# Expert 0's weights fetched in 16 half pieces through two buffers, and the operand copies of the attention stage issued later

## The chip, the cores and the metric

The kernel runs on one core of a Trainium2 chip, as one launch. The metric is the device time of one execution in microseconds (us). TensorE is called PE below, VectorE DVE, ScalarE ACT, GpSimd POOL and SyncE SP; SP's own queue issues nearly all transfers of the stage in question.

## The reference

Three layers follow one another. The first is causal attention of 4 batches with 8 heads, 576 positions and 64 features, whose scores get a bias made from a running sum of `max(s, 0)`:

```python
cum = np.cumsum(np.maximum(s, 0.0), axis=-1)
bias = -(cum[:, :, :, None] - cum[:, :, None, :])
scores = np.where(causal, -1000000000.0, scale * q @ k.T + np.minimum(bias, 0.0))
attn = np.exp(scores - scores.max(-1)); attn = attn / (attn.sum(-1) + 1e-09)
out = attn @ v
```

Its output, 2304 tokens of 512 features, goes through a mixture of 8 experts: each token takes the expert of its largest gate logit, computes `relu(x @ w1[e]) @ w2[e]` (512 to 1024 to 512) and is scaled by two gates. The last layer is `relu(x @ w_in)**2 @ w_out` (512 to 2048 to 512). All inputs are float32, and w_in and w_out arrive as 64-bit words that the kernel converts itself.

## The kernel before

**Attention.** The 32 heads are worked on two at a time, so there are 16 pairs, numbered 0 to 15 here. A pair has seven units (a block of 128 queries of one or both heads, or the last 64 queries of both, the tail unit). For each unit PE multiplies queries with keys (`emit_s`, line 472), DVE adds the mask and finds the maximum (`emit_m`), ACT takes the exponentials (`emit_e`), PE transposes them (`emit_t`), ACT or DVE copies them out of PSUM (`emit_v`), and PE multiplies with the values (`emit_pv`).

**Operand tiles.** Queries and keys are held as a rounded part and a remainder, each a float32r number. For pairs from 2 on, ACT and DVE write both parts of both heads into one tile `sta` (three buffers, used in turn). Three transfers then copy head 1's rows into a second tile `stb` (two buffers), `spread_b`; after them two transfers overwrite the copied rows of `sta` with head 0's rows, `spread_a`. Four small transfers (`load_aug`) bring the bias rows into both tiles. The first score product of a pair needs the end of all of these. Since `spread_a` writes rows that `spread_b` reads, it may be issued only when the moves of `spread_b` have landed.

**What sets the order.** Every step is put into a list with a due time in units, seven per pair, and the list is sorted by it (`at`, `emit_tasks`). The sorted order is the program's order on every engine and queue; a due time is not a time on the chip. The numbers in the table `K_` are these due times. Of them `dup` is the due time of `spread_b` and `dupa` that of `spread_a`, both counted from the start of the pair ahead (`t0`):

```python
tb = t0 + max(K_["dup"], K_["qk"][2] + K_["qkl"] - early(pp) + 0.4)
at(tb - 0.05, load_aug, pp, 1)
at(tb, spread_b, pp)
at(tb - K_["dup"] + K_["dupa"], spread_a, pp)
```

For each pair SP issues, beside these, three transfers of values (line 362 and 365), four of raw queries and keys two to three pairs ahead (335 and 338), and two that store the attention's output of an earlier pair (708 and 712). SP works in order: a transfer that waits holds up all behind it.

**Expert 0's weights.** During pairs 8 to 15 the kernel also prepares the weights of the first expert, 4 MB in 8 pieces of 512 KB. Each is fetched into the buffer `stg` (line 224, one buffer of 128x1024), rounded by ACT into the first half of the weight tile (233), and POOL subtracts this from the raw piece to get the remainder (237). A piece is due every 6.88 units, its transfer 3.5 units ahead of ACT's cast. ACT works in order too, so that a cast that waits for its piece holds up the exponentials behind it.

The experts and the last layer follow; there the weights of later experts are prepared with other buffers and by DVE. `w_lo` and `w_job` serve both stages.

Of the kernel before, what the change touches and what calls it, by code (L numbers as in the profile page):

```python
# [12 lines left out]
F32 = mybir.dt.float32  # L13
# [6 lines left out]
ALU = mybir.AluOpType  # L20
# [4 lines left out]
P = 128  # L25
# [4 lines left out]
K_ = dict(  # L30
    S=3,
    O=0,
    pbufs=4,
    NO=5,
    od=[-1.86, -0.33],
    lorder=[0, 2, 11, 10, 3, 1, 4],
    lvact=[[0], [1], [0], [1], [1], [0], [1, 0]],
    lpv=[[7.65, 7.66], [4.06, 5.56, 6.05, 6.9, 7.45]],
# [17 lines left out]
    qk=[-3.45, -2.16, -1.89],  # L56
    qkh=0.61,
    qkl=0.65,
    dup=-3.2,
    dupa=-0.7,  # L60
    pv=[[3.74, 3.87], [8.47, 8.49, 8.51, 8.53, 8.57]],
    ovact=[1, 1],
    gk=[4.59, 4.65, 5.02, 5.22, 5.65, 6.55, 7.35, 7.38, 7.54, 8.68, 9.78, 10.48, 10.95, 11.72, 12.72, 14.11, 14.46, 14.36, 14.48, 14.97, 15.87, 16.25, 17.18, 17.4, 19.12, 20.76],
# [5 lines left out]
    w0=6.88,  # L69
# [17 lines left out]
def attention_moe_ffn_kernel(  # L87
# [14 lines left out]
    nc = tc.nc  # L102
# [9 lines left out]
    NPAIR = B * HP  # L112
# [50 lines left out]
    halves = {}  # L163
# [18 lines left out]
    def raw_src(key, i):  # L182
        e, ab = key
        if ab == "a":
            if e == 0:
                return w1[e, i * P:(i + 1) * P, :]
            if e < E:
                return w1.rearrange("e k f -> (e k) f")[ds(reg_e[e] * DM + i * P, P), :]
            c = (e - E) * FE
            return w_in[i * P:(i + 1) * P, c:c + FE]  # L190
        r = 2 * i * P
        if e == 0:
            return w2[e, r:r + 2 * P, :].rearrange("(k p) d -> p k d", p=P)
        if e < E:
            return w2.rearrange("e f d -> (e f) d")[ds(reg_e[e] * FE + r, 2 * P), :].rearrange("(k p) d -> p k d", p=P)
        r += (e - E) * FE
        return w_out[r:r + 2 * P, :].rearrange("(k p) d -> p k d", p=P)
# [11 lines left out]
    def at(key, fn, *args):  # L209
        tasks.append((key, len(tasks), fn, args))  # L210

    def emit_tasks(before=None):
        tasks.sort(key=lambda t: (t[0], t[1]))
        while tasks and (before is None or tasks[0][0] < before):
            _, _, fn, args = tasks.pop(0)
            fn(*args)

    raw = {}
# [8 lines left out]
    def w_parts(job):  # L227
        key, i = job
        w = halves[key]
        return w[:, 0, i * 1024:(i + 1) * 1024], w[:, 1, i * 1024:(i + 1) * 1024]  # L230
# [3 lines left out]

    def w_lo(job):
        hi, lo = w_parts(job)
        (nc.gpsimd if job[0][0] == 0 else nc.vector).tensor_tensor(out=lo, in0=raw.pop(job), in1=hi.bitcast(F32), op=ALU.subtract)  # L237

    def w_job(job, t_load, t_hi, t_lo):
        if job not in raw:  # L240
            at(t_load, w_load, job)
        at(t_hi, w_hi, job)
        at(t_lo, w_lo, job)

    def half_jobs(e, ab):
        return [((e, ab), i) for i in range(4)]
# [31 lines left out]
    with tc.manual_schedule():  # L278
        with ExitStack() as actx:
# [1 line left out]
            cq_p = actx.enter_context(tc.tile_pool(name="cq", bufs=1))  # L281
            qk_p = actx.enter_context(tc.tile_pool(name="qk", bufs=2))
            qr_p = actx.enter_context(tc.tile_pool(name="qr", bufs=1))
            stg_p = actx.enter_context(tc.tile_pool(name="stg0", bufs=1))
            v_p = actx.enter_context(tc.tile_pool(name="v", bufs=3))
            p_p = actx.enter_context(tc.tile_pool(name="p", bufs=K_["pbufs"]))
            sm_p = actx.enter_context(tc.tile_pool(name="sm", bufs=6))
# [583 lines left out]
            with tc.tile_pool(name="prep", bufs=1) as prep:  # L871
# [19 lines left out]
                    out=mf, in_=zf[:, 0:P], pattern=[[-1, P]], compare_op=ALU.is_ge, fill=NEG, base=0,  # L891
                    channel_multiplier=1)
                nc.vector.tensor_copy(out=mask[:, 3 * P:4 * P], in_=mf)
                for hd in range(2):
# [4 lines left out]
                    out=mt, in_=of[:, 0:P], pattern=[[1, P]], compare_op=ALU.is_gt, fill=0.0, base=0,  # L899
# [5 lines left out]
                    out=sel.unsqueeze(2), in_=ident.rearrange("p (g r) -> p r g", r=NH)[:, 0:2 * ND], axis=AX.X, op=ALU.add)  # L905
                nc.vector.tensor_scalar(out=sq, in0=sq, scalar1=0.0, scalar2=None, op0=ALU.max)
                nc.vector.tensor_tensor_scan(
                    out=cum, data0=cum_r[0:NH].bitcast(F32), data1=sq, initial=0.0, op0=ALU.mult, op1=ALU.add)
# [5 lines left out]
                    out=cum_k[NH:2 * NH], in0=cum, in1=cum_k[0:NH].bitcast(F32), op=ALU.subtract)  # L914
# [26 lines left out]
                for r in range(1, 2 * ND):  # L941
                    nc.vector.tensor_scalar(
                        out=cum_q[:, r], in0=cum_r.bitcast(F32), scalar1=sel[:, r:r + 1], scalar2=None, op0=ALU.mult)
# [7 lines left out]
                    out=aug_d[0:2].rearrange("c r t -> (c r) t"), in_=cum_r[0:2 * NH].bitcast(F32))  # L951
# [40 lines left out]
            NU = len(order)  # L992
# [60 lines left out]
            for b in range(B):  # L1053
# [4 lines left out]
                        at(tl + K_["lt"][half][i], fn, b, half)  # L1058
                tg = NU * (NPAIR - 1) + K_["lpv"][0][-1] + K_["xe"]
                emit_gate(b, tg + 0.01 if last else NU * HP * (b + 1) + K_['go'], K_["gk"])  # L1060
            for i, job in enumerate(half_jobs(0, "a") + half_jobs(0, "b")):
                tw = NU * NPAIR - K_["w0"] * (8 - i)
                w_job(job, tw - 3.5, tw, tw + 1)
            emit_tasks()

        stg_p = ctx.enter_context(tc.tile_pool(name="stg", bufs=3))
# [338 lines left out]
        for g in range(E):  # L1405
            n0 = g * NF
            at(n0 + NF + 1.5, emit_yv, g)
            at(n0 + NF + 1.8, y_store, g)
            if g + 1 < E:
                for c in range(len(rows_of(g + 1))):  # L1410
                    x_trans(g + 1, c, n0 + K_['xt0'] + K_['xt1'] * c, 0.3)
            if g + 2 < E:
                at(n0 + 6.5, gather, g + 2)
            hj = half_jobs(g + 1, "a") + half_jobs(g + 1, "b")
            at(n0 + 2.15, alloc_next)
            at(n0 + 2.15, alloc_next)
            for i, job in enumerate(hj):
                ta = n0 + 2.2 + i
                if g + 1 == E and i >= 6:
                    continue  # L1420
                w_job(job, max(ta - K_["wld"], -0.7), ta + K_['wh'], ta + K_['wl'])
# [6 lines left out]
        if wide:  # L1428
            for n in range(NCV):
                t = K_['cvp'] * n + K_['cv0']  # L1430
# [34 lines left out]
        for i, job in enumerate(half_jobs(E, "b")[2:4]):  # L1465
            w_job(job, 0.55 + 0.1 * i, 1.3 + i, 1.6 + i)
        if wide:
            for i, n in enumerate(range(NCV, len(pieces))):
                t = 2.1 * i + 1.5
# [16 lines left out]
        with tc.For_i(0, end, 1):  # L1486
# [5 lines left out]
            for b in range(B):  # L1492
                for t in range(NB):
                    r1 = lp.tile([P, P], F32, tag="or1", name="or1")
                    nc.vector.tensor_scalar(
                        out=r1, in0=it_f, scalar1=rc[:, b, t:t + 1], scalar2=None, op0=ALU.is_equal)
# [3 lines left out]
                        out=vv[:, 2], in0=oh_all[:, b, t], scalar1=gsq[:, b, t:t + 1], scalar2=None, op0=ALU.mult)  # L1500
# [40 lines left out]
            for e in range(E):  # L1541
                xr = xr_p.tile([P, CH, DM], F32, tag="xr", name="xr")
                nc.gpsimd.indirect_dma_start(
                    out=xr[:, 0, :], out_offset=None, in_=x_d[:, :],
# [8 lines left out]
                    out=out[:, :], out_offset=bass.IndirectOffsetOnAxis(ap=jx[:, e:e + 1], axis=0), in_=oo,  # L1553
# [30 lines left out]
```

## Time and profile before

| what | value |
|---|---|
| time, median of 3 runs | 953.6 us (952.04 to 953.99) |
| the profiled execution | 956.37 us, span 954.7 us, mean granted clock 0.959 |
| busy share of the span | PE 92%, DVE 56%, ACT 46%, POOL 30% |
| attention stage | up to about 265 us of the span |
| transfers of the SP queue | 103.77 MB, 39.7% of the 16 DMA engines' span |

A busy share is a mean over stages with different limits. In the attention stage all five engines and the SP queue hand work to one another, so there the chain of waits and the queue's own timeline tell more than shares. Times in rows are microseconds from the start of the span.

### The profile page before, as it was taken

The page shows a single profiled execution, that of the slowest core. Times are in us where ns is not written, and L with a number is a line of the kernel's source. Part 1 is how long each engine was busy: PE and PEld are TensorE (multiplying, and loading weights), DVE is VectorE, ACT ScalarE, POOL GpSimd, SP SyncE. Part 2 cuts the span into 40 slices and gives each one's busy share as a digit, 9 for nine tenths or more (in the row PEclk, how much of TensorE's full clock was granted, in tenths as well). Part 3 has the DMA queues.
Part 4 walks back from the last instruction along what each step waited for, and adds up shares of the span by engine and source line. Part 5 has one row for each costly group of instructions (what it writes and reads, how often), then busy time and mean ns, then how long its engine had stood idle before and what let it go on. Part 6 is the DMA issues. An engine that isn't in the chain of part 4 may idle for free.

```text
span 954.7 us, 15017 instructions
## 1 busy us (share of the span) xinstructions
PE 874.5 (92%) x5397; PEld 766.2 (80%) x5397; DVE 530.1 (56%) x1182; ACT 439.4 (46%) x961; POOL 281.8 (30%) x285
## 2 busy tenths in 40 slices
PE   7999967779989998998989899999999999999990
PEld 5777745656668998998988789999999999999980
DVE  8776834557766768877986866332323322322220
ACT  6787744658725554664663544332322322322220
POOL 5432322233234567667751234110000001001001
PEclk9999977889999999998998999999999999999995
DMA  5787866666237888898897433110000100000001
GB/s 147 167 188 178 189 136 141 144 171 163 82 100 226 277 232 255 256 281 271 251 298 232 149 138 142 67 67 2 33 32 23 45 1 34 1 1 34 1 1 36
DMA packets 86933, 123.88 MB, mean 130 GB/s; under 512 B 33473, under 2 KB 58049, under 8 KB 85954
## 3 DMA queue, kind: packets, MB, share of 16 engines
q1 hardware_dynamic: 80338, 103.77, 39.7%
q0 software_dynamic: 6224, 18.01, 5.2%
q10 hardware_dynamic: 288, 1.05, 0.3%
q8 instruction: 45, 0.74, 0.3%
q14 instruction: 38, 0.31, 0.1%
HBM read 83.12 MB, written 23.17 MB: 111 GB/s over the span
## 4 chain that ended last, share of the span: by engine, by line
PE 67%; DMA 12%; DVE 5%; ACT 4%; issue 4%; SPq 3%; POOL 2%; POOLq 0%; DVEq 0%; ACTq 0%
PE z L1176 27%; PE z L1221 19%; PE z L1214 8%; DMA stg<-in_moe_w_dram 4%; PE s L472 4%; PE t L570 3%; PE t L532 3%; DMA xr<-x_d,tbl_p 1%; ACT p L516 1%; DMA stg<-w_in_d 1%; PE z L1102 1%; DMA cv<-in_moe_w_in_dram 1%; DVE w L237 1%; PE s L608 1%; PE t L386 1%
## 5 line engine op out<-in xcount | busy, mean ns | idle before, releaser
L1176 PE MATMUL z<-xt,w 128*128 128x384 f32 (+6 forms) x1920 | 339.1, 326 | 7.2 <-DVE h L1188 3.6
L1176 PEld LDWEIGHTS z<-xt,w 128*128 128x128 f32 x1920 | 315.8, 191 | 17.9 <-DVE r L1194 3.9
L1221 PE MATMUL z<-w,h 128*128 128x512 f32 x864 | 215.1, 393 | 0.4 <-ACT ysb L1235 0.4
L1221 PEld LDWEIGHTS z<-w,h 128*128 128x128 f32 x864 | 160.8, 188 | 29.9 <-ACT ysb L1235 0.8
L1194 DVE SCALAR_TENSOR_TENSOR r<-z,r 128x384 f32<-128x384 f32 x96 | 53.4, 556 | 166.1 <-ACT r L1193 166.1
L1214 PE MATMUL z<-h,w 128*128 128x304 f32 (+5 forms) x768 | 120.6, 307 | 8.7 <-DVE ysb L1233 7.4
L233 ACT CAST w<-stg 128x1024 fp32r<-128x1024 f32 x80 | 84.1, 1051 | 96.6 <-DMA stg<-in_moe_w_dram 75.2
L1193 ACT ACTIVATE r<-z 128x384 f32<-128x384 f32 x96 | 47.0, 489 | 162.7 <-PE z L1176 162.7
L1214 PEld LDWEIGHTS z<-h,w 128*128 128x128 f32 x768 | 112.1, 195 | 10.4 <-DVE ysb L1233 8.3
L1254 POOL DMA_INDIRECT out_dram<-ysb,tok_m x18 | 17.6, 976 | 321.9 <-ACT ysb L1243 289.6
L237 DVE TENSOR_TENSOR w<-stg,w 128x1024 fp32r<-128x1024 f32 x72 | 108.4, 1505 | 7.1 <-ACT w L233 7.0
L1197 DVE TENSOR_TENSOR h<-r,h 128x384 fp32r<-128x384 f32 x96 | 55.7, 580 | 55.6 <-ACT h L1196 55.6
L516 ACT ACTIVATE p<-p,nm 128x128 f32<-128x128 f32 (+3 forms) x144 | 84.3, 590 | 3.9 <-DVE nm L499 3.8
L499 DVE CUSTOM_DVE_ANT_0 p<-s,mask 128x128 f32<-128x128 f32 (+3 forms) x128 | 59.8, 486 | 45.8 <-PE s L472 38.5
L1196 ACT CAST h<-r 128x384 fp32r<-128x384 f32 x96 | 49.2, 513 | 76.9 <-DVE r L1194 76.9
L532 PE MATMUL t<-ident,p 128*128 128x128 f32 x400 | 70.5, 291 | 12.7 <-ACT p L516 11.8
L1158 POOL TENSOR_TENSOR cvm<-cvm,cva 128x512 f32<-128x512 f32 x32 | 44.9, 1404 | 102.0 <-DVE cva L1157 66.3
L532 PEld LDWEIGHTS t<-ident,p 128*128 128x128 f32 x400 | 47.4, 146 | 26.8 <-ACT p L516 19.4
L1159 POOL TENSOR_TENSOR cvm<-cvs,cvm 128x512 f32<-128x512 f32 x32 | 58.1, 1815 | 2.5
L570 PE MATMUL t<-pt,v 128*64 128x320 f32 (+4 forms) x448 | 53.8, 371 | 0.1
L472 PE MATMUL s<-sta 68*128 68x192 f32 (+7 forms) x204 | 50.9, 347 | 2.0 <-DVE pt L553 0.7
L551 ACT COPY pt<-t 128x512 f32<-128x512 f32 (+1 forms) x94 | 46.7, 514 | 9.7 <-PE t L532 5.5
(217 smaller groups left out, 952.6 us busy)
## 6 DMA issues: line engine op xcount, KB each, us to landing
stg<-in_moe_w_dram SPq DMA_DIRECT2D x64, 512.0 KB
cv<-in_moe_w_out_dram SPq DMA_DIRECT2D x16, 512.0 KB
stb<-sta SPq DMA_DIRECT2D x14, 576.0 KB
cv<-in_moe_w_in_dram SPq DMA_DIRECT2D x14, 512.0 KB
xr<-yT_d SPq DMA_DIRECT2D x6, 768.0 KB
q<-in_q_dram SPq DMA_DIRECT2D x16, 256.0 KB
k<-in_k_dram SPq DMA_DIRECT2D x16, 256.0 KB
v<-in_v_dram SPq DMA_DIRECT2D x32, 128.0 KB
```

Source lines behind the costliest of these rows:

```text
L233: nc.scalar.copy(out=w_parts(job)[0], in_=raw[job])
L237: (nc.gpsimd if job[0][0] == 0 else nc.vector).tensor_tensor(out=lo, in0=raw.pop(job), in1=hi.bitcast(F32), op=ALU.subtract)
L472: nc.tensor.matmul(ps[0:mw, d0:d0 + nn], lhsT=ql[r, m0:m0 + mw], rhs=kl[r, c0:c0 + nn], start=(i == 0 and (tail or n == 0)), stop=(done an ...
L499: nc.vector.tensor_tensor_reduce(out=dst, in0=src, in1=msk, scale=-1.0, scalar=3.0e38, op0=ALU.add, op1=ALU.min, accum_out=nm[:, c:c + 1])
L516: nc.scalar.activation(out=pt[:, cs], in_=pt[:, cs], func=AF.Exp, scale=-1.0, bias=nm[:, c:c + 1], accum_out=rs[:, r:r + 1])
L532: nc.tensor.transpose(tp[:, i * P:(i + 1) * P], pt[:, j0:j0 + P], ident)
L570: nc.tensor.matmul(o[64 * hd:64 * hd + 64, c0:n], lhsT=vt[r0:P, jb, hd, :], rhs=pt[r0:P, hd, jb, c0:n], start=(jb == 0), stop=(jb == last))
L1159: nc.gpsimd.tensor_tensor(out=m, in0=sq, in1=m, op=ALU.add)
L1176: nc.tensor.matmul(ps[:, 0:n], lhsT=wa[:, zw, kk, fl * P:(fl + 1) * P], rhs=xt[:, zx, kk, 0:n], start=(i == 0), stop=(i == 3 * KD - 1))
L1197: nc.vector.tensor_tensor(out=ht[:, 1, 0:n], in0=gg, in1=ht[:, 0, 0:n].bitcast(F32), op=ALU.subtract)
L1214: nc.tensor.matmul(y_acc[g][d][:, 0:n], lhsT=wb[:, zw, fl, d * P:(d + 1) * P], rhs=ht[:, zh, 0:n], start=(f == 0 and i == 0), stop=(f == n ...
L1221: nc.tensor.matmul(acc, lhsT=ht[:, zh, c * P:(c + 1) * P], rhs=wb[:, zw, fl, :], start=(f == 0 and i == 0), stop=(f == nf - 1 and i == 2))
```

## The change

The eight pieces of expert 0 become sixteen of 256 KB, one due every 3.44 units, in two buffers of 128x512 (the same bytes). A transfer is due 5 units ahead of its cast, and POOL's subtraction half a unit behind the cast in place of one unit. `dup` goes from -3.2 to -2.3 and `dupa` from -0.7 to -0.2: the copies to `stb` are due 0.9 units later, those within `sta` 0.5 units later. For pair 2 the other term of the maximum decides, so that there only `spread_a` moves. Line numbers behind line 258 grow by 17.

```diff
-    dup=-3.2,
-    dupa=-0.7,
+    dup=-2.3,
+    dupa=-0.2,
...
     def w_lo(job):
         hi, lo = w_parts(job)
-        (nc.gpsimd if job[0][0] == 0 else nc.vector).tensor_tensor(out=lo, in0=raw.pop(job), in1=hi.bitcast(F32), op=ALU.subtract)
+        nc.vector.tensor_tensor(out=lo, in0=raw.pop(job), in1=hi.bitcast(F32), op=ALU.subtract)
...
+    def part_views(key, i, h):
+        c = slice(i * 1024 + h * 512, i * 1024 + (h + 1) * 512)
+        return halves[key][:, 0, c], halves[key][:, 1, c]
+
+    def part_load(key, i, h):
+        t = stg_p.tile([P, 512], F32, tag="stg", name="stg")
+        src = raw_src(key, i)
+        nc.sync.dma_start(out=t, in_=src[:, h * 512:(h + 1) * 512] if key[1] == "a" else src[:, h, :])
+        raw[key, i, h] = t
+
+    def part_hi(key, i, h):
+        nc.scalar.copy(out=part_views(key, i, h)[0], in_=raw[key, i, h])
+
+    def part_lo(key, i, h):
+        hi, lo = part_views(key, i, h)
+        nc.gpsimd.tensor_tensor(out=lo, in0=raw.pop((key, i, h)), in1=hi.bitcast(F32), op=ALU.subtract)
...
-            stg_p = actx.enter_context(tc.tile_pool(name="stg0", bufs=1))
+            stg_p = actx.enter_context(tc.tile_pool(name="stg0", bufs=2))
...
-            for i, job in enumerate(half_jobs(0, "a") + half_jobs(0, "b")):
-                tw = NU * NPAIR - K_["w0"] * (8 - i)
-                w_job(job, tw - 3.5, tw, tw + 1)
+            for i, job in enumerate((k, i, h) for k, i in half_jobs(0, "a") + half_jobs(0, "b") for h in range(2)):
+                tw = NU * NPAIR - K_["w0"] / 2 * (16 - i)
+                at(tw - 5.0, part_load, *job)
+                at(tw, part_hi, *job)
+                at(tw + 0.5, part_lo, *job)
```

The order of PE's and DVE's instructions stays as it was. On SP, before the weights begin, this stood for one pair (`v` values, `stb` and `sta` the operand tiles, `x_d` the store of an earlier pair, `q` and `k` raw operands):

```order
L365 DMA v<-in_v_dram 64x2x64
L375 DMA stb_135<-aug_d 4x576
L376 DMA stb_135<-aug_d 4x576
L423 DMA stb_135<-sta_132 64x2304
L423 DMA stb_135<-sta_132 64x576 x2
L708 DMA x_d<-xs 128x4x128
L712 DMA x_d<-xs 64x128
L335 DMA q<-in_q_dram 128x2x256
L338 DMA q<-in_q_dram 64x2x64
L335 DMA k<-in_k_dram 128x2x256
L338 DMA k<-in_k_dram 64x2x64
L423 DMA sta_132<-sta_132 64x576 x2
```

After the change the same pair reads, on SP:

```order
L382 DMA v<-in_v_dram 64x2x64
L725 DMA x_d<-xs 128x4x128
L729 DMA x_d<-xs 64x128
L352 DMA q<-in_q_dram 128x2x256
L355 DMA q<-in_q_dram 64x2x64
L352 DMA k<-in_k_dram 128x2x256
L355 DMA k<-in_k_dram 64x2x64
L392 DMA stb_135<-aug_d 4x576
L393 DMA stb_135<-aug_d 4x576
L440 DMA stb_135<-sta_132 64x2304
L440 DMA stb_135<-sta_132 64x576 x2
L440 DMA sta_132<-sta_132 64x576 x2
```

The store and the four raw operand transfers went ahead of the copies to `stb`; nothing stands any more between these and the copies within `sta`. Between two visits to `sta` SP issues the same transfers as before.

On SP around the first weight piece, before (the pair whose tile is `sta_132` is pair 9):

```order
L338 DMA k<-in_k_dram 64x2x64
L224 DMA stg<-in_moe_w_dram 128x1024
L423 DMA sta_132<-sta_132 64x576 x2
L375 DMA sta_132<-aug_d 4x576
L376 DMA sta_132<-aug_d 4x576
L362 DMA v<-in_v_dram 128x4x64 x2
```

And after, for the same pair (the first row `stg` is the second half piece, the other one the third):

```order
L440 DMA stb_136<-sta_132 64x576 x2
L252 DMA stg<-in_moe_w_dram 128x512
L440 DMA sta_132<-sta_132 64x576 x2
L392 DMA sta_132<-aug_d 4x576
L393 DMA sta_132<-aug_d 4x576
L252 DMA stg<-in_moe_w_dram 128x512
L379 DMA v<-in_v_dram 128x4x64 x2
```

The first half piece stands one pair further ahead, between `sta` of pair 8 and the values. So each pair has one half piece behind its `sta` copies and one between the copies to `stb` and those within `sta` of the next. On ACT the first piece's cast keeps its place, and the second half's cast comes a good half pair later, ahead of the tail unit's exponentials:

```order
L533 ACTIVATE p,rs_150<-p,nm 128x384
L433 CAST sta_134<-t 128x512
L598 COPY oTx<-t 128x256
L256 CAST w_309<-stg 128x512
L533 ACTIVATE p,rs_150<-p,nm 128x576
```

Before, no cast of a weight stood between the copy of `oTx` and that exponential.

## Rows read from the trace of the kernel before

**Rows 1.** Windows: before, during and after the first four weight pieces; busy time of each engine.

```profile
core 0: us, PE busy (x) PEld busy (x) DVE busy (x) ACT busy (x) POOL busy (x), PEclk, DMA share, GB/s
50.00:115.00 65.00, 63.93 (x512) 47.84 (x508) 49.07 (x175) 50.44 (x147) 19.59 (x26) 1.00 0.79 181
120.00:215.00 95.00, 68.86 (x466) 50.84 (x466) 45.51 (x168) 49.93 (x141) 27.02 (x28) 0.82 0.64 148
215.00:262.00 47.00, 45.29 (x361) 31.87 (x363) 35.12 (x123) 36.50 (x104) 14.45 (x15) 1.00 0.50 125
```

**Rows 2.** Waits in 120 to 262 us: total, times, longest, in us.

```profile
ACT w L233 <- DMA stg<-in_moe_w_dram: 34.5, 6, 10.3
```

**Rows 3.** Chain of waits, 118 to 230 us: start, length, what.

```profile
118.13 1.89 DMA sta<-aug_d
...
129.47 6.41 DMA stg<-in_moe_w_dram
...
223.87 4.61 DMA stg<-in_moe_w_dram
```

**Rows 4.** Timeline of SP, one pair before the weights: start, length, transfer.

```profile
76.06 1.24 SPq L423 DMA_DIRECT2D sta<-sta  x2
...
80.28 0.44 SPq L375 DMA_DIRECT2D stb<-aug_d  x1
...
81.16 3.47 SPq L423 DMA_DIRECT2D stb<-sta  x3
84.72 0.78 SPq L708 DMA_DIRECT2D x_d<-xs  x1
...
86.46 0.73 SPq L335 DMA_DIRECT2D q<-in_q_dram  x1
...
89.25 2.00 SPq L423 DMA_DIRECT2D sta<-sta  x2
```

**Rows 5.** Timeline of SP: the copies within `sta` of pairs 3, 8 and 9, first piece.

```profile
49.77 1.24 SPq L423 DMA_DIRECT2D sta<-sta  x2
...
116.31 1.24 SPq L423 DMA_DIRECT2D sta<-sta  x2
...
129.47 0.59 SPq L224 DMA_DIRECT2D stg<-in_moe_w_dram  x1
130.10 1.14 SPq L423 DMA_DIRECT2D sta<-sta  x2
```

**Rows 6.** Timeline of PE: first score products of pairs 8, 12 and 15.

```profile
120.15 0.45 PE L472 MATMUL s<-sta 68*128 68x192 f32 x2 [0.52 <-DMA sta<-aug_d]
...
206.17 0.45 PE L472 MATMUL s<-sta 68*128 68x192 f32 x2
...
246.03 0.45 PE L472 MATMUL s<-sta 68*128 68x192 f32 x2
```

**Rows 7.** Tile `stg`: casts and subtractions, ns least/median/most.

```profile
L233 ACT CAST w<-stg x69: 1037/1052/1082, 135.9 to 519.7; 128x1024 fp32r<-128x1024 f32 x69
...
L237 POOL TENSOR_TENSOR w<-stg,w x8: 2352/2364/2372, 137.0 to 250.8; 128x1024 fp32r<-128x1024 f32 x8
```

**Rows 8.** Timeline of SP, pair 15.

```profile
233.94 3.56 SPq L423 DMA_DIRECT2D stb<-sta  x3
...
238.99 0.78 SPq L712 DMA_DIRECT2D x_d<-xs  x1
240.00 1.10 SPq L423 DMA_DIRECT2D sta<-sta  x2
```

**Rows 9.** Waits of the SP queue, 232 to 243 us.

```profile
SPq L423 <- DMA stb<-sta: 0.2, 1, 0.2
```

**Rows 10.** Timeline of SP: a store and a query transfer with little issued ahead.

```profile
191.35 0.39 SPq L335 DMA_DIRECT2D q<-in_q_dram  x1
...
244.38 0.38 SPq L708 DMA_DIRECT2D x_d<-xs  x1
```

**Rows 11.** Chain of waits: tail units' score products of pairs 13 and 15.

```profile
232.80 1.06 PE s L472 x8
...
256.69 1.07 PE s L472 x8
```

## The prediction

> **What bounds the kernel now.** I read the windows by stage first, then the waits of the stretch in which the weights are prepared, then the chain of waits there, and last the timelines of SP and of PE's first score products, since the chain kept leading into SP.
>
> The windows show two regimes in one stage [rows 1]. From 50 to 115 us PE is busy 63.93 of 65 us at a granted clock of 1.00. From 120 to 215 us, where expert 0's pieces come in, it is busy 68.86 of 95 us and the clock's mean is 0.82, a mix of its levels of 1.2 and 2.4 GHz. Behind that, PE is full again. ACT's wait for the weight pieces is the largest there that a transfer ends: 34.5 us in six waits, the longest 10.3 us [rows 2]. The chain shows why: the first 512 KB piece lands 6.41 us after its issue, a later one, in a quieter stretch, 4.61 us [rows 3]. While ACT stands at its cast, the exponentials behind it stand too, and PE and SP with them.
>
> The first regime is not as safe as its busy share suggests. SP has one pair's transfers back to back: the copies to `stb` start at 80.28 and run to 84.63, the store and the raw operands fill the time to 89.25, and `sta` follows at once [rows 4]. From pair 3 to pair 9 the copies within `sta` go from 49.77 to 130.10 us, 80.33 us for six pairs, 13.39 us each [rows 5]. At pair 8 PE's first score product starts at 120.15 us, 0.13 us after the last `sta` transfer landed (118.13 + 1.89) [rows 3, 6]. So by then SP paces PE, and a microsecond more per pair on SP is a microsecond more per pair of time.
>
> **The weight pieces.** ACT reached the first cast at 125.6 us: the piece landed at 129.47 + 6.41 = 135.88, less the wait of 10.3 [rows 2, 3]. That is 5.4 us behind the score product of pair 8. In the new order the first half piece is issued right behind pair 8's last `sta` transfer, the one of 118.13, and lands 4.6 to 6.4 us later if a half takes as long as a whole piece does. It is there before the cast or about with it. Each even piece stands so. Each odd piece is issued just ahead of the next pair's copies within `sta`. These need from their issue to the landing of their bias rows 120.02 - 116.31 = 3.7 us, and a wait and a transfer's issue stand ahead of them, so the odd piece lands at about the time at which PE could start that pair at all. I take the waits for pieces as gone. What is late next is SP.
>
> The halves cost 16 issues for 8. One issue took 0.59 us [rows 5]; I charge that for a half also, which makes 1.18 us per pair on SP. On ACT 16 casts take between the same sum and twice 1.05 us per old piece, so 0 to 1.05 us more per pair, on POOL likewise 0 to 2.4 us [rows 7]. ACT is busy 50 of 95 us in that stretch and POOL 27 [rows 1]. Both sit beside PE's wait for SP; I charge nothing, and at worst, uncovered, ACT's 1.05 us per pair.
>
> **The later copies.** The order shows that between two visits to `sta` SP issues just what it did, but the copies to `stb` now stand directly ahead of the ones within `sta`, which must not be issued before the first two moves of the former have landed. Until now a store and four raw operand transfers covered that time, 84.72 to 89.25 us, 4.5 us [rows 4]. The nearest rows for the bare wait are those of pair 15, with no raw operands in between: the moves' issue ends at 233.94 + 3.56 = 237.50, the store's at 239.77, and the first `sta` copy goes out at 240.00, after a wait of 0.2 us that ends with the moves' landing [rows 8, 9]. Landing thus comes 2.4 to 2.5 us after the issue's end. From below the wait is 0: a 9 KB transfer landed 1.89 us after its issue began [rows 3], and the second move's issue begins earlier than the end of the third's by more than that if the third takes most of the 3.56 us. From above: the piece behind the raw operands took 6.41 us and the one behind copies 4.61 us, so that raw operands ahead may add 1.8 us, which makes 4.2 us. I take 2.4 us, the value that was seen directly.
>
> A part comes back. With less in flight, a store's first transfer took 0.38 us where 0.78 us was usual, a query's 0.39 us against 0.73 us [rows 4, 10]. The store and the raw operands no longer follow the long moves; between 0 and some 1.0 us per pair, if the second and third transfers gain as well, I take 0.5 us.
>
> The Trainium skill says on this (DMA: Bandwidth & Descriptors, "Two DMAs through the same engine are not ordered") that sharing a queue gives no order between two dependent transfers, and that the issuing engine has to wait for the first one's semaphore. By this rule the wait stands on SP and the sum below holds; if order in the queue were enough, the third rival's time would come out. The wait of 0.2 us before pair 15's `sta` [rows 9] agrees with the rule, though a row so small is thin support.
>
> **The sum**, against the profiled execution of 956.37 us (span 954.7 us):
>
> 1. Pairs 3 to 8, before any piece: 6 x (2.4 - 0.5) = 11.4 us lost. Pair 8's first score product goes from 120.15 to 131.6 us. Nothing covers it, since the 0.13 us of slack there is all there is.
> 2. Pairs 9 to 12, with raw operands and two half pieces: 13.39 + 1.18 + (2.4 - 0.59, the odd piece's issue lying inside the wait) - 0.5 = 15.88 us each, 63.5 us. Before, PE's score products of pairs 8 and 12 lay 206.17 - 120.15 = 86.0 us apart [rows 6]. 22.5 us won.
> 3. Pairs 13 to 15: no raw operands are left to load, 15.88 - 2.79 (86.46 to 89.25 [rows 4]) = 13.09 us each, 39.3 us, against 246.03 - 206.17 = 39.9 us. 0.6 us won.
> 4. From there to the end all stays: PE paces the last pair, and experts and last layer have their order unchanged.
>
> Together 11.7 us won: 944.7 us against the profiled execution. The median of the runs shown, 953.6 us, is 2.8 us below that execution, so I forecast 953.6 - 11.7 = 941.9, told as 942 us. The low clock of 120 to 215 us is inside the 86.0 us; in the new pairs PE has some 12 us of work in 15.9 us, so a stretch at 1.2 GHz behind a wait for SP would mostly fill time in which PE waits.
>
> **Rivals.**
>
> *The spreads' wait is dearer, and the kernel gets slower.* The place is SP between the copies to `stb` and within `sta`, in 13 pairs. Every microsecond beyond my 1.9 us net costs 13 us, so from 0.9 us more (a wait of 3.3 us) the gain is gone. At the upper bound of 4.2 us the sum is -11.7 + 13 x 1.8 = +11.7: 965 us. For it speaks that the raw operands now stand in the queue just ahead, and that the DMA engines are 79% busy there [rows 1]. Against it, that SP's pause lets them drain. Chance 0.20.
>
> *The casts still wait.* If the odd pieces land late, because the three moves to `stb` stand ahead of them, ACT stands in each of eight pairs with the tail's exponential behind it. At 1.5 us per pair that is 12 us, and 954 us comes out: no change. Against it: even a whole piece's 6.41 us would end about when `sta` has landed (0.59 + 1.8 + 3.7 = 6.1 us). Chance 0.13.
>
> *The later copies cost nothing.* If the moves have landed by the time SP is through with the third, term 1 is 0, term 2 is 4 x (13.39 + 1.18) = 58.3 us, 27.7 won, and in term 3 PE sets the pace: tail products of pairs 13 and 15 lie 256.69 - 232.80 = 23.9 us apart [rows 11], 11.95 us per pair, 35.9 us for three, 4.0 won. 922 us. For it speaks only the lower bound above. Chance 0.17.
>
> **How the numbers follow.** My own case has 0.50; with the wait between 1.9 and 2.9 us its range is 936 to 949. The range for 8 in 10, 925 to 958 us, leaves out most of the third rival and the upper half of the first. About 0.2% (1.9 us) is what a measurement of this kernel can tell from no change. Faster: 0.49 of my case, 0.17 of the third rival, 0.02 of the second, 0.68. Same: 0.06 of the second, 0.03 from the edges of the others, 0.09. Slower: 0.18 of the first and 0.05 of the second, 0.23.
>
> **What would show it.** In the new profile, SP should wait about 2 us for the moves to `stb` ahead of each copy within `sta`, from pair 3 on; these copies should come 15.3 us apart up to pair 8, and pair 8's first score product at 131 to 132 us (a start near 120 us would refute term 1). ACT's waits for pieces should fall from 34.5 us to a few. Pair 12 should start at 195 us, pair 15 at 234 us. I am wrong if ACT's waits stay above 15 us, or if SP's wait is under 1 or over 3.3 us. Behind the attention stage no duration should change.

## The result

The changed kernel takes 937.6 us, the median of four runs (935.23 to 939.28), against 953.8 us before on the same chip: a ratio of 0.9832, 95% interval 0.9802 to 0.9862. That is 16.2 us less; 942 us was forecast, 11.7 us less.

The profiled execution took 935.23 us with a span of 933.5 us, 21.2 us below the one before. The windows of the same stretches as in [rows 1], for the changed kernel:

```profile
core 0: us, PE busy (x) PEld busy (x) DVE busy (x) ACT busy (x) POOL busy (x), PEclk, DMA share, GB/s
50.00:115.00 65.00, 60.59 (x447) 45.66 (x444) 42.94 (x148) 45.26 (x129) 16.49 (x18) 0.95 0.69 161
120.00:215.00 95.00, 85.32 (x642) 63.40 (x639) 62.06 (x223) 68.63 (x198) 39.16 (x44) 0.95 0.78 189
215.00:262.00 47.00, 44.16 (x358) 30.19 (x356) 34.81 (x143) 28.80 (x86) 11.84 (x18) 1.00 0.35 91
```

The reader is to see both halves of the sum in them. From 50 to 115 us PE did less than before, 447 matmuls for 512. From 120 to 215 us it did more, 642 for 466, and the granted clock rose from 0.82 to 0.95.

ACT's waits for the pieces in 120 to 262 us, answering [rows 2] (total, times, longest, in us):

```profile
ACT w L256 <- DMA stg<-in_moe_w_dram: 3.0, 2, 1.9
```

And SP's waits for the moves to `stb` in the attention stage, answering [rows 9], in the same columns:

```profile
SPq L440 <- DMA stb<-sta: 20.7, 15, 2.9
```

The 34.5 us of waits for pieces are gone, and 20.7 us of a wait that was 0.2 us have come. The timeline of SP shows it (start, length, transfer): the copies within `sta` of pair 3, then pairs 5 and 6, then pair 8. It answers to [rows 4, 5, 8]:

```profile
51.32 1.10 SPq L440 DMA_DIRECT2D sta<-sta  x2
...
74.22 3.67 SPq L440 DMA_DIRECT2D stb<-sta  x3
80.87 1.10 SPq L440 DMA_DIRECT2D sta<-sta  x2
...
84.63 0.59 SPq L725 DMA_DIRECT2D x_d<-xs  x1
85.27 0.51 SPq L729 DMA_DIRECT2D x_d<-xs  x1
85.88 0.54 SPq L352 DMA_DIRECT2D q<-in_q_dram  x1
...
89.43 3.75 SPq L440 DMA_DIRECT2D stb<-sta  x3
95.90 1.10 SPq L440 DMA_DIRECT2D sta<-sta  x2
...
119.31 3.64 SPq L440 DMA_DIRECT2D stb<-sta  x3
124.82 1.10 SPq L440 DMA_DIRECT2D sta<-sta  x2
```

Between 77.89 and 80.87 SP issues nothing, 2.98 us, and again 2.72 us up to 95.90; up to 124.82 it is 1.87 us. Those of pairs 5 and 6 are the longest: over pairs 4 to 8 this gap is 2.28 us in the mean. From the `sta` copies of pair 3 to those of pair 8 SP took 124.82 - 51.32 = 73.50 us, 14.70 us per pair, where it had taken 116.31 - 49.77 = 66.54 us, 13.31 us per pair [rows 5]. Without the gaps that is 12.42 us, so the issuing itself fell by 0.9 us per pair. PE's first score products of pairs 8, 12 and 15, answering [rows 6]:

```profile
128.46 0.45 PE L489 MATMUL s<-sta 68*128 68x192 f32 x2 [1.92 <-DMA sta<-aug_d]
...
189.52 0.71 PE L489 MATMUL s<-sta 68*128 68x192 f32 x2 [2.25 <-DVE sta L437]
...
229.13 0.45 PE L489 MATMUL s<-sta 68*128 68x192 f32 x2
```

And the chain of waits that leads to the first of them (start, length, what):

```profile
119.87 4.93 DMA stb<-sta
...
126.55 1.77 DMA sta<-aug_d
...
128.46 0.86 PE s L489 x4
```

Pair 8 starts 8.3 us later than before, and at its start the chain runs through the landing of the moves to `stb`. Pair 12 starts 16.7 us earlier, pair 15 16.9 us. From there to the end it took 704.4 us (933.5 less 229.1) against 708.7 us (954.7 less 246.0). Over the ten other profiles of this study that stretch, in which only the last weight pieces are ordered differently, lay between 706.3 and 710.3 us. About half of these 4.3 us lies inside that spread. Most of the difference is PE's own time: for 3870 matmuls each it was busy 660.3 us from 229 to 933 us, at a mean granted clock of 0.98, where it had been busy 663.7 us from 246 to 954 us, at 0.97. Why the clock was higher stays open. So the attention stage gave 16.9 of the 21.2 us, near the 16.2 us by which the medians differ.

### The profile page after: what moved, and what is told of

The parts are those of the page before. It is cut to its first block, busy times and chain, and to the rows that moved or that the text cites. A ratio compares the mean times of both kernels' runs of the same rounds, so it can differ in the third digit from the quotient of the medians.

```text
span 933.5 us, 15073 instructions
## 1 busy us (share of the span) xinstructions
PE 868.6 (93%) x5397; PEld 762.7 (82%) x5397; DVE 533.5 (57%) x1182; ACT 440.8 (47%) x969; POOL 282.7 (30%) x293
## 4 chain that ended last, share of the span: by engine, by line
PE 60%; DMA 14%; DVE 8%; ACT 5%; issue 4%; POOL 3%; SPq 1%; POOLq 0%; DVEq 0%; ACTq 0%
PE z L1195 23%; PE z L1240 19%; PE z L1233 4%; PE s L489 4%; DMA stb<-sta 3%; DVE w L237 3%; PE t L587 3%; DMA cv<-in_moe_w_in_dram 3%; PE t L549 3%; ACT p L533 2%; DMA w_out_d<-cvm 1%; PE t L403 1%; DMA sta<-aug_d 1%; DMA stg<-in_moe_w_dram 1%; POOL cvm L1177 1%
## 5 line engine op out<-in xcount | busy, mean ns | idle before, releaser
L1233 PE MATMUL z<-h,w 128*128 128x304 f32 (+5 forms) x768 | 118.7, 304 | 9.3 <-DVE ysb L1252 7.4
L237 DVE TENSOR_TENSOR w<-stg,w 128x1024 fp32r<-128x1024 f32 x72 | 110.5, 1535 | 7.9 <-ACT w L233 7.7
L233 ACT CAST w<-stg 128x1024 fp32r<-128x1024 f32 x72 | 75.5, 1050 | 67.0 <-DMA stg<-in_moe_w_dram 46.2
L489 PE MATMUL s<-sta 68*128 68x192 f32 (+7 forms) x204 | 52.9, 357 | 15.2 <-DMA sta<-aug_d 11.1
L568 ACT COPY pt<-t 128x512 f32<-128x512 f32 (+1 forms) x94 | 46.8, 514 | 11.4 <-PE t L549 5.6
```

What stands on the lines that cost most here:

```text
L233: nc.scalar.copy(out=w_parts(job)[0], in_=raw[job])
L237: nc.vector.tensor_tensor(out=lo, in0=raw.pop(job), in1=hi.bitcast(F32), op=ALU.subtract)
L489: nc.tensor.matmul(ps[0:mw, d0:d0 + nn], lhsT=ql[r, m0:m0 + mw], rhs=kl[r, c0:c0 + nn], start=(i == 0 and (tail or n == 0)), stop=(done an ...
L1233: nc.tensor.matmul(y_acc[g][d][:, 0:n], lhsT=wb[:, zw, fl, d * P:(d + 1) * P], rhs=ht[:, zh, 0:n], start=(f == 0 and i == 0), stop=(f == n ...
```

## The experiments

Two theories were set against each other at first. A: the early pieces win, and the later copies cost a bare wait on SP, that is, a wait during which SP has nothing else to issue. B: the later copies are what wins, since SP then no longer stands before PE's tail product. All ratios are to the kernel before, run on the same chip.

| kernel | time, us | ratio, 95% interval |
|---|---|---|
| the change | 937.6 | 0.9832 (0.9802 to 0.9862) |
| half pieces ahead, old copies | 926.5 | 0.9714 (0.9681 to 0.9747) |
| later copies alone | 947.6 | 0.9938 (0.9912 to 0.9965) |
| whole pieces 5 units ahead, nothing else | 921.5 | 0.9662 (0.9634 to 0.969) |
| the change, raw operands behind the copies | 923.2 | 0.969 (0.9653 to 0.9728) |
| half pieces at 3.5 units, old copies | 942.3 | 0.9881 (0.9832 to 0.993) |
| the change with 3.5 units | 943.1 | 0.9881 (0.984 to 0.9923) |
| whole pieces 4.25 units ahead | 922.5 | 0.9667 (0.9627 to 0.9708) |
| whole pieces 5 units ahead, copies covered | 918.6 | 0.9629 (0.9591 to 0.9667) |
| whole pieces 3.5 units ahead, copies covered | 926.5 | 0.974 (0.9678 to 0.9802) |

**The half pieces without the later copies.** Against the changed kernel:

```diff
-    dup=-2.3,
-    dupa=-0.2,
+    dup=-3.2,
+    dupa=-0.7,
```

> The sixteen half pieces kept, the operand copies at their old due times (dup -3.2, dupa -0.7). Theory A (the early half pieces win, the later copies cost a bare wait on SP of about 2 us per pair): no wait of SP for the moves to stb, pair 8's first score product back at about 120 us in place of 128.5, pairs 9 to 12 some 14.6 us each, the time 922 to 932 us. Theory B (the later copies are what wins, since SP no longer stands before the stb copies until PE's tail product is done): SP's wait there comes back with 15 us or more, ACT waits for pieces again, 943 us or more.

Measured 926.5 us. PE's first score products of pairs 8, 12 and 15:

```profile
121.63 0.45 PE L489 MATMUL s<-sta 68*128 68x192 f32 x2 [0.44 <-DMA sta<-aug_d]
...
182.12 0.45 PE L489 MATMUL s<-sta 68*128 68x192 f32 x2
...
219.25 0.45 PE L489 MATMUL s<-sta 68*128 68x192 f32 x2
```

Pair 8 is back near its old start, and pairs 9 to 12 (from the start of pair 8 to that of pair 12) take 15.1 us each, where 14.6 us were expected. The time lies inside theory A's range. SP waits 1.9 us for PE's tail products, not 15 us. Theory B's forecast fails: on top of early half pieces the later copies cost 0.9832 - 0.9714 = 1.2%, about 11 us.

**The later copies alone.** Against the kernel before:

```diff
-    dup=-3.2,
-    dupa=-0.7,
+    dup=-2.3,
+    dupa=-0.2,
```

> The later operand copies alone (dup -2.3, dupa -0.2), weights in eight whole pieces through one buffer as before. Theory A: pair 8 starts about 8 us later than in the kernel before, ACT's waits for the pieces stay at 25 us or more, 953 to 965 us. Theory B: the waits for pieces shrink to a few us, 940 us or less.

Measured 947.6 us, 0.6% faster than before: it lies in neither theory's range. ACT's waits for pieces, 110 to 250 us, lie between the two as well, at 13.7 us:

```profile
ACT w L233 <- DMA stg<-in_moe_w_dram: 13.7, 4, 5.5
```

The first score products of pairs 8, 12 and 15 show where the time went:

```profile
128.05 0.45 PE L472 MATMUL s<-sta 68*128 68x192 f32 x2 [1.67 <-DMA sta<-aug_d]
...
195.56 0.45 PE L472 MATMUL s<-sta 68*128 68x192 f32 x2
...
235.65 0.45 PE L472 MATMUL s<-sta 68*128 68x192 f32 x2 [1.70 <-DMA sta<-aug_d]
```

The loss before pair 8 is there as expected, 7.9 us. But pairs 9 to 12 take 67.5 us in place of 86.0 us. So the old pieces gain from the later copies, beside a bare wait on SP of 36.4 us. The kernel before says why. First its SP's waits for PE's tail products, 30 to 262 us:

```profile
SPq L375 <- PE s L472: 27.0, 8, 7.2
```

Then its timelines: SP up to the second piece, ACT's first cast, and PE behind it, down to the tail unit's products with `stb`:

```profile
133.39 0.65 SPq L365 DMA_DIRECT2D v<-in_v_dram  x1
142.85 0.27 SPq L375 DMA_DIRECT2D stb<-aug_d  x1
...
143.57 3.61 SPq L423 DMA_DIRECT2D stb<-sta  x3
...
151.98 0.54 SPq L224 DMA_DIRECT2D stg<-in_moe_w_dram  x1
...
135.89 1.04 ACT L233 CAST w<-stg 128x1024 fp32r<-128x1024 f32 x1 [10.28 <-DMA stg<-in_moe_w_dram]
...
137.47 0.63 PE L665 MATMUL t<-oTx,wp 128*32 128x256 f32 x1 [8.43 <-ACT pt L551]
...
141.75 1.31 PE L472 MATMUL s<-stb 128*128 128x288 f32 x4
```

Before, SP stood from 134.0 to 142.9 us in front of the copies to `stb`, which wait for PE's tail product in the other user of that tile; PE waited for ACT, and ACT for the first piece. The second piece stood behind those copies on SP. So each late piece made the next one late, 22.5 us from piece to piece (129.47 to 151.98). With the later copies a piece stands ahead of them, and SP's waits for PE's products in front of them are gone; in that kernel's timeline the first two pieces go out 16.6 us apart:

```profile
133.32 0.59 SPq L224 DMA_DIRECT2D stg<-in_moe_w_dram  x1
134.01 0.28 SPq L375 DMA_DIRECT2D stb<-aug_d  x1
...
149.88 0.54 SPq L224 DMA_DIRECT2D stg<-in_moe_w_dram  x1
```

The piece still stands behind the raw operands there, and ACT still waits for it. My account had the late pieces right but not this ring. The later experiments take it up.

**The lead alone.** One number against the kernel before:

```diff
-                w_job(job, tw - 3.5, tw, tw + 1)
+                w_job(job, tw - 5.0, tw, tw + 1)
```

> The kernel before with one number changed: the whole pieces are due 5 units ahead of their casts in place of 3.5. Theory A in the form that the lead alone decides: the piece is issued right behind the copies within sta, lands within 6.4 us and about with ACT's cast, waits for pieces under 8 us in sum, pairs 9 to 12 about 14 us each, 924 to 934 us. Rival (size and second buffer are needed too, as a whole piece lands too late or waits for its buffer): waits for pieces of 15 us or more, 940 us or more.

Measured 921.5 us, 2.5 us below the expected range and 1.7 points of the ratio better than the whole change. SP's timeline around the first piece:

```profile
116.34 1.24 SPq L423 DMA_DIRECT2D sta<-sta  x2
...
118.51 0.36 SPq L224 DMA_DIRECT2D stg<-in_moe_w_dram  x1
```

ACT's timeline, the first cast (no idle time is noted in front of it):

```profile
125.54 1.04 ACT L233 CAST w<-stg 128x1024 fp32r<-128x1024 f32 x1
```

PE's first score products of pairs 8, 12 and 15:

```profile
120.19 0.45 PE L472 MATMUL s<-sta 68*128 68x192 f32 x2 [0.51 <-DMA sta<-aug_d]
...
176.18 0.78 PE L472 MATMUL s<-sta 68*128 68x192 f32 x2 [0.39 <-DMA sta<-aug_d]
...
213.66 0.45 PE L472 MATMUL s<-sta 68*128 68x192 f32 x2
```

The piece goes out 11 us earlier than before (129.47) and is there when ACT comes. Pairs 9 to 12 take 14.0 us each. Neither halves nor a second buffer are needed. The copies to `stb` keep their due time here, and yet SP's waits for PE's tail products, 30 to 262 us, are down from 27.0 us:

```profile
SPq L375 <- PE s L472: 1.5, 4, 0.4
```

So with the piece on time the rest of the ring goes too.

**The raw operands put behind the copies.** Against the changed kernel:

```diff
-    ldqk=-16.83,
+    ldqk=-16.23,
```

> The changed kernel, with the raw queries and keys due 0.6 units later, so that their four transfers stand between the copies to stb and those within sta again (2.8 us of issue). Theory A: the bare wait on SP goes from about 20 us in sum to under 6 us, pair 8 starts at 120 to 123 us, 925 to 932 us. Theory B (SP's order does not matter, the gain and loss lie elsewhere): within 3 us of the changed kernel's 937.6 us.

Measured 923.2 us, under the expected range by 2 us. SP's wait for the moves in the attention stage:

```profile
SPq L440 <- DMA stb<-sta: 3.4, 3, 1.4
```

PE's first score product of pair 8:

```profile
119.00 0.45 PE L489 MATMUL s<-sta 68*128 68x192 f32 x2
```

With four transfers in between, 17 of the 20.7 us of bare wait go, and 1.4 points of the ratio with them. So all that the later copies cost comes back by SP's order alone.

**Halves without the lead.** Against the half pieces with old copies, `tw - 5.0` becomes `tw - 3.5`:

```diff
-                at(tw - 5.0, part_load, *job)
+                at(tw - 3.5, part_load, *job)
```

> Sixteen half pieces in two buffers, but due 3.5 units ahead as before, and the operand copies at their old due times: the size and the buffers alone. Theory A (the lead, that is the place in SP's order, decides): the even pieces stand behind the raw operands again, ACT waits for pieces 15 us or more in sum, 936 to 946 us. Rival (halves and a second buffer would do): waits under 8 us, 931 us or less.

Measured 942.3 us. ACT's waits for pieces, 120 to 250 us:

```profile
ACT w L256 <- DMA stg<-in_moe_w_dram: 23.1, 7, 8.5
```

SP's waits for PE's tail products, 30 to 262 us:

```profile
SPq L392 <- PE s L489: 14.3, 5, 4.9
```

As theory A expected. Size and buffers bring 1.2% of their own, but waits for pieces and SP's wait for PE stay. Which of the two, size or buffer, brings that was not taken apart.

**The change with the old lead.** The same edit against the changed kernel.

> The changed kernel with its half pieces due 3.5 units ahead in place of 5, the later copies kept. Theory A: even pieces stand behind the raw operands but ahead of the copies to stb, so that casts wait somewhat, beside SP's bare wait: pair 8 near 128 us, 939 to 947 us. Rival (with the later copies the lead no longer matters, as SP paces each pair): within 3 us of 937.6 us.

Measured 943.1 us. Waits for pieces 20.2 us (eight, of 3.7 us at most), SP's bare wait 28.4 us. The time lies inside theory A's range, but not far enough from 937.6 us to rule out the rival for certain: with the later copies the lead of 5 units is worth some 0.5 points (0.9881 to 0.9832, and the intervals overlap); without them it is worth 1.7 points (0.9881 to 0.9714).

**A lead between.** `tw - 4.25` in the kernel before.

> The kernel before with its whole pieces due 4.25 units ahead, half way between 3.5 and 5. In SP's order they then stand behind or ahead of the values, but ahead of the copies to stb. Theory A in the form that it matters only whether a piece stands ahead of the copies to stb, which wait for PE's tail product: 919 to 926 us, as with 5 units. Rival (the gain goes with the lead's length): half of the gain, 932 to 940 us.

Measured 922.5 us: all of the gain, as theory A said. On SP the first piece goes out at 121.41 us, behind the values and ahead of the copies to `stb` at 122.82 us. With the copies at their old place, what counts is on which side of them a piece stands in SP's order. It is not all that can make a piece late: with the later copies and the lead of 3.5 units, in whole pieces or in halves, a piece stands ahead of the copies but behind the raw operands, and ACT waits 13.7 and 20.2 us for pieces.

**The old lead, with the piece ahead of the copies.** Against the kernel before, with the 3.5 units, the whole pieces and the one buffer kept:

```diff
-    dup=-3.2,
-    dupa=-0.7,
+    dup=-2.3,
+    dupa=-0.2,
...
-    ldqk=-16.83,
+    ldqk=-16.23,
```

> The kernel before with its whole pieces, one buffer and its lead of 3.5 units; only the copies to stb and the raw queries and keys are due later, so that in SP's order a piece stands ahead of the copies to stb, right behind the stores, and the raw operands still cover the moves. Theory (the loss before came from the piece standing behind SP's wait for PE's tail product; the lead counts only through the place): the piece goes out at about 122 us and lands 4.6 to 6.4 us later against a cast reached at 125.6 us, so waits of 1 to 3 us per piece, 925 to 933 us. Rival (the later copies help the old pieces only by lengthening every pair, as the copies alone gave 947.6 us, or the lead's number itself decides): 940 us or more.

Measured 926.5 us. SP around the first piece:

```profile
120.58 0.59 SPq L224 DMA_DIRECT2D stg<-in_moe_w_dram  x1
121.27 0.29 SPq L375 DMA_DIRECT2D stb<-aug_d  x1
...
129.44 1.18 SPq L423 DMA_DIRECT2D sta<-sta  x2
```

From 120 to 250 us ACT waits 3.5 us for pieces, and SP no longer waits for PE's tail products in front of the copies to `stb`. The weight code is that of the kernel before to the letter; only its neighbours in SP's queue moved. The time lies inside the range that the theory gave. This shows the ring directly: with the piece ahead of SP's wait for PE, most of the loss of [rows 2] goes.

**Both cures together.** The last edit and `tw - 5.0` in the kernel before.

> Best guess: whole pieces due 5 units ahead, later copies, raw queries and keys due 0.6 units later so that their transfers cover the moves to stb. Expected: no wait for pieces to speak of, SP's bare wait under 6 us, pair 8 at 119 us, pairs 9 to 12 about 13.9 us each, 916 to 922 us. If pairs 9 to 12 are paced by PE and ACT by now, no better than the 921.5 us of the lead alone.

Measured 918.6 us, the fastest of the study. Pair 8 starts at 120.3 us, pairs 9 to 12 take 13.4 us each, and SP's bare wait is 5.8 us, much as expected. Its interval overlaps that of the lead alone, so that it beats the kernels before and after for certain, but not the change of one number.

## Why the prediction was right

The sign, the two places and their order of size held, and so did the wait, the step on which the sum stood. The sizes of two terms were off, both toward too long a pair.

- *The waits for pieces go.* 3.0 us of 34.5 us are left, in two casts. All other pieces, even and odd, were on time, as the prediction worked out from the landing times.
- *Term 1, the bare wait up to pair 8.* 8.3 us were lost, 11.4 us forecast. The wait is there: 1.87 to 2.98 us in pairs 4 to 8, 2.28 us in the mean, for the 2.4 us taken. What was mis-sized is what comes back: SP's issuing fell by 0.9 us per pair (13.31 to 12.42), and I took 0.5 us, the middle of my bounds; the upper bound of 1.0 us was nearer.
- *Term 2, pairs 9 to 12.* 189.52 - 128.46 = 61.1 us, or 15.3 us each, against 15.88 us forecast and 86.0 us before. The gain was 24.9 us for 22.5 us. Here the saving was as taken, and the rest was cheaper: from the end of the moves' issue to the `sta` copies SP took 2.06 us in the mean, the odd piece's issue inside, where the sum has 2.4 us, and the even piece's issue took 0.36 us in place of 0.59 us. What is left of a pair took 12.84 us, where the sum has 13.39 - 0.5 = 12.89 us. It would have been less without one query issue of 2.46 us, in place of 0.53 us, in the first of these pairs; why it was so long is not shown.
- *Term 3, pairs 13 to 15.* 39.6 us, forecast 39.3 us.
- *The rest of the program.* The prediction had it unchanged. The two profiles differ by 4.3 us, 2 us more than the other profiles spread, and the cause of these 2 us stays open. The medians, on which the forecast rests, show little of it: they differ by 16.2 us.

Together 16.9 us, forecast 11.7 us. The first rival named the place, but the price stayed under its turning point. The second did not come. The third, later copies that cost nothing, would have given 922 us: taking the copies back gave 926.5 us and covering them 923.2 us. By the ratios that is 11 and 14 us off the changed kernel, so the 20 us between 942 and 922 us priced the bare wait too dear, which is the error of terms 1 and 2 once more. The Trainium skill says that a dependent transfer must wait on its issuing engine (DMA: Bandwidth & Descriptors, "Two DMAs through the same engine are not ordered"). The trace agrees in that SP does stand there, 20.7 us in all, where the prediction had one wait of 0.2 us to go by; no run leaves the wait out, so none shows that it is needed.

One reason was incomplete without spoiling the forecast: the prediction took the old loss for a late transfer with ACT behind it. It was a ring of piece, ACT, PE's tail product, SP and next piece, and the later copies open this ring by themselves. That is why they alone won 0.6% where theory A expected no gain.

## What to carry to other kernels

When a transfer is late, look at what stands ahead of it in its queue before making it smaller or double-buffering it: here one due time, which put it ahead of a wait for another engine, was worth more than the whole change. When two dependent transfers move in an in-order queue, keep independent issues between them that are as long as the first one's landing. And judge parts of a change apart: these two each helped the kernel before, and together they lost 11 us to the better one alone.

## What the runs showed of the hardware

A transfer's issue on SP is not a fixed price. The same store and query transfers took 0.59, 0.51 and 0.54 us in the changed kernel where [rows 4, 8] show 0.78 us for either store and 0.73 us for the first query. With the same list of transfers SP needed 0.9 us less per pair. By these runs the price goes mostly with what stands close ahead in the queue, and the low one needs no pause of SP. In the run with the raw operands behind the copies SP hardly waits for the moves, and there the store, behind the values, takes 0.54 us, while the first query, now behind the long moves, takes 0.78 us:

```profile
66.62 0.65 SPq L382 DMA_DIRECT2D v<-in_v_dram  x1
67.37 0.54 SPq L725 DMA_DIRECT2D x_d<-xs  x1
...
69.44 3.62 SPq L440 DMA_DIRECT2D stb<-sta  x3
73.16 0.78 SPq L352 DMA_DIRECT2D q<-in_q_dram  x1
```

Waits of PE of some 2 us can go with a lower clock. In the changed kernel PE waited for a pair's operands for 1.88 us up to 69.33 us and for 1.98 us up to 99.53 us, and right behind these waits it ran at 1.2 GHz: the granted clock was 0.50 from 70 to 73 us and from 101 to 103 us, and 1.00 again from 74 and from 104 us. In the kernel before, with no wait above 0.71 us in front of a matmul from 50 to 115 us, it stayed at 1.00. It does not follow each time: behind the wait of 1.92 us up to 128.46 us the granted clock was 1.00 up to 140 us. No cost shows in SP's pace: the two pairs with the lower clock took 15.21 and 14.13 us from `sta` to `sta`, the other three up to pair 8 took 14.34, 15.03 and 14.79 us.
